# Sparse attention, gate and mixer in one kernel: gate preparation placed inside the mixer of the batch ahead, gate values in tiles of their own, the second batch's convolution mostly on ScalarE and GpSimd

## The chip, the cores and the metric

The kernel runs on one core of a Trainium2 chip. The metric is the time of one execution on the device in microseconds (us); lower is better. PE is TensorE (PEld its weight loads), DVE is VectorE, ACT is ScalarE, POOL is GpSimd and SP is SyncE, whose queue issues the DMAs.

## What is computed

Three stages follow each other. B = 4 batches, H = 8 heads, S = 576 positions, head width 64, model width D = 512. Everything is float32.

```python
# attention: only the 32 largest scores of a row count
scores = 0.125 * q @ k.T                      # [4, 8, 576, 576]
kth    = the 32nd largest of each row
attn   = softmax(where(scores >= kth, scores, -1e9))
x      = attn @ v                             # heads side by side: [4, 576, 512]
# gate: a causal convolution of 5 taps along the positions, per channel
gate   = sigmoid(sum_k conv_w[k] * x[s - 4 + k])
x      = (gate * (x @ w_val)) @ w_out
# mixer
u      = x + (relu(x.T @ w_tok1) @ w_tok2).T
out    = u + relu(u @ w_ch1) @ w_ch2          # inner width 1536
```

## The kernel before

**Attention.** The heads are taken in pairs, 16 in all, four to a batch (`p = 4 b + c`). A pair has five units `u` of 128 rows of each head (the last unit holds 64 rows of both). For a unit, PE computes the scores into PSUM (`scores`, L366, L387, L389), ACT copies them to SBUF (L377, L395), and DVE finds the 32nd largest value of each row: `fold` (L531) halves the row by maxima and minima, `topk` (L544 to L546) takes the best of the halves, and `top32` (L567, L569) runs four rounds of MAX and three of MATCH_REPLACE for each tile. Then ACT forms a large penalty W for scores under the threshold (L469), POOL subtracts it (L471, `E <- S, W`), ACT takes the exponential (L474), PE transposes E (L483), ACT copies the transposes to `pT` (L488), and PE multiplies with v (`pv`, L496 to L501). Two units are held and their products issued in one group; ACT copies the result to `xf[c]` (L504). For the last six pairs the scores are computed early and parked in DRAM through the tiles `pst` (`pre`), which are free again after that.

**Gate preparation.** `prep(b, c)` handles channel block c (128 of the 512 channels) once its pair is done: reciprocal of the row sums (L685 to L696), their spread over the channels by PE (L694, L700, L703) into two of the three PSUM banks `mo`, the multiplication of `xf[c]` by them on DVE (L708, L710), the split of x into a high and a low part (`split`, L586 on ACT, L587 on POOL), and the convolution. For the first batch the convolution is done by PE with diagonal matrices (L723). For the other three it runs in the single PSUM bank Q: for each half of 288 positions ACT writes the first tap (L732), DVE adds four more (L735, each reading and writing Q), and ACT takes the tanh (L737) into the tile `f[c]`.

**Gate and mixer.** All weight products are three passes over high and low parts (`mm3`, L647 to L649). `gate(b)` computes `x @ w_val` (96 passes of 288 columns), DVE combines it with the gate value (L764), the result is split and multiplied by `w_out` (96 more), and ACT writes it to `f[c]` (L770). `mix(b)` transposes `f`, does the two token products, and then G = 3 rounds of four `ch1` blocks with ReLU and four `ch2` blocks, whose sums DVE adds to `f` (L789). So in this kernel the gate values of a batch and the mixer's running result of the batch before stand in the same four tiles `f`. In batches one and two (`b in LO` is false) the low parts of the mixer are formed by ACT and POOL through two tiles `t`, in three and four by DVE.

**Order.** Nothing is issued directly: each step is recorded as an operation with its engine, a cost and the buffers it reads and writes. `Order.issue` then lists all operations by priorities (list scheduling on estimated costs, refined in 8 rounds), to which the table `SHIFT` adds corrections by operation number. Each engine works through its own list strictly in that order. Buffers and PSUM banks are assigned in recording order, so where a step is recorded decides what it has to wait for: in `all`, a batch's four `prep` calls are recorded after its last pair and after the mixer of the batch before, then its `gate`, then its `mix`; attention of the next batch is recorded after that and listed among them by priority. A `check` near the end tests that the shortened selection was valid; a complete version of the program behind a branch is not taken.

## Time and profile before

| what | value |
|---|---|
| time, median of 3 runs | 877.21 us (875.7 to 878.32) |
| profiled execution: time / span | 874.26 us / 872.4 us |
| busy: PE / DVE / ACT / POOL | 820.0 / 743.1 / 602.0 / 386.8 us |
| mean granted TensorE clock | 0.978 of full speed |
| DMA | 139.4 MB, 160 GB/s |
| chain that ended last | PE 62%, DVE 27%, ACT 7% |

The span runs from the first to the last instruction of the profiled execution; the time of that execution also holds what lies around it. Busy time is the union of an engine's instructions. Matmuls overlap in the pipeline and their ends are modelled, so that a stretch in which PE is busy throughout can still hold a few per cent of lost time; what the table of stages shows best is where PE stood still. The granted clock is the share of full speed that TensorE got: 1.0 is 2.4 GHz, and it falls to 1.2 GHz (0.5) for some stretches.

### The profile page before, as it was taken

Reading aid. Unit: us, or ns where it says so; the run is one execution under the profiler, and the core shown is the slowest. Engines: PE = TensorE matmul, PEld = TensorE weight load, DVE = VectorE, ACT = ScalarE, POOL = GpSimd, SP = SyncE. Lnnn points to the kernel's source line nnn. Section 1 sums busy time; section 2 is a strip of 40 time slices with the busy share of each in tenths; the row PEclk is TensorE's granted clock in tenths of the full one; section 3 lists DMA queues with packets and bytes.
Section 4 is the critical chain, followed back from the end, with each engine's and each line's share of the span. In section 5 each row is a group of like instructions: output and inputs, shape, how many; then the busy total and the mean of one; then the engine's idle time right before and its main releaser. Section 6 shows DMA issues by size and latency. Waiting matters only on the chain.

```text
span 872.4 us, 19037 instructions
## 1 busy us (share of the span) xinstructions
PE 820.0 (94%) x6585; PEld 711.0 (81%) x6585; DVE 743.1 (85%) x2786; ACT 602.0 (69%) x1484; POOL 386.8 (44%) x372
## 2 busy tenths in 40 slices
PE   6898897899999999979999999998999999999997
PEld 3564565589789888769798888988899998889997
DVE  7999999999789999999999989999999995623222
ACT  5999999976777759677987778587876655432110
POOL 1344354467676748345784454454354223302000
PEclk8899999999999999979999999999999999999999
DMA  6445445558246764636433336735346645233553
GB/s 236 162 143 178 164 160 187 188 174 302 84 139 220 251 196 155 197 123 186 131 103 90 98 94 198 240 121 172 113 152 206 190 146 151 98 97 96 172 169 107
DMA packets 45835, 139.38 MB, mean 160 GB/s; under 512 B 5216, under 2 KB 5472, under 8 KB 45728
## 3 DMA queue, kind: packets, MB, share of 16 engines
q1 hardware_dynamic: 45728, 138.06, 48.8%
q8 instruction: 54, 0.88, 0.4%
q14 instruction: 53, 0.43, 0.2%
HBM read 100.62 MB, written 37.42 MB: 158 GB/s over the span
## 4 chain that ended last, share of the span: by engine, by line
PE 62%; DVE 27%; ACT 7%; issue 2%; DMA 1%; POOL 1%; SPq 0%; DVEq 0%; ACTq 0%
PE mo L647 14%; PE mo L648 12%; PE mo L649 12%; PE PT L483 5%; DVE top L567 5%; DVE Z L569 5%; PE PT L496 4%; PE Sp L366 4%; DVE Q L735 4%; DVE y L531 3%; DVE X L544 2%; DVE Sp L531 1%; PE mo L366 1%; DVE A L531 1%; ACT E L474 1%
## 5 line engine op out<-in xcount | busy, mean ns | idle before, releaser
L647 PE MATMUL mo<-r,ring 128*128 128x288 f32 x864 | 266.6, 309 | 3.0 <-DVE f L789 1.0
L648 PE MATMUL mo<-r,ring 128*128 128x288 f32 x864 | 255.5, 296 | 0.4 <-POOL r L587 0.2
L649 PE MATMUL mo<-r,ring 128*128 128x288 f32 x864 | 255.3, 296 | 0.0
L471 POOL TENSOR_TENSOR E<-S,W 128x576 f32<-128x576 f32 x144 | 202.8, 1424 | 98.8 <-ACT W L469 63.6
L647 PEld LDWEIGHTS mo<-r,ring 128*128 128x128 f32 x864 | 162.9, 189 | 17.3 <-issue 8.9
L648 PEld LDWEIGHTS mo<-r,ring 128*128 128x128 f32 x864 | 163.1, 189 | 0.9 <-POOL r L587 0.8
L649 PEld LDWEIGHTS mo<-r,ring 128*128 128x128 f32 x864 | 162.9, 189 | 0.0
L567 DVE MAX8 top<-Z 128x8 f32<-128x168 f32 x432 | 127.2, 322 | 0.6
L474 ACT ACTIVATE E<-E,nb 128x576 f32<-128x576 f32 x144 | 112.2, 780 | 14.6 <-POOL E L471 14.2
L483 PE MATMUL PT<-ident,E 128*128 128x128 f32 x656 | 102.8, 286 | 12.9 <-ACT pT L488 5.7
L488 ACT ACTIVATE pT<-PT 128x512 f32<-128x512 f32 (+1 forms) x144 | 94.9, 659 | 28.7 <-PE PT L483 27.7
L469 ACT ACTIVATE W<-S,nb 128x576 f32<-128x576 f32 x144 | 108.2, 776 | 0.3 <-POOL E L471 0.3
L483 PEld LDWEIGHTS PT<-ident,E 128*128 128x128 f32 x656 | 76.9, 145 | 35.9 <-ACT pT L488 12.0
L569 DVE MATCH_REPLACE8 Z<-top,Z 128x168 f32<-128x168 f32 x288 | 89.8, 317 | 0.0
L556 POOL TENSOR_TENSOR bad<-X,top 128x6 f32<-128x6 f32 (+1 forms) x80 | 16.2, 203 | 160.9 <-DVE top L567 142.2
L496 PE MATMUL PT<-pT,v 128*64 128x128 f32 (+1 forms) x640 | 78.9, 266 | 4.1 <-ACT pT L488 3.8
L497 PE MATMUL PT<-pT,v 128*64 128x128 f32 (+1 forms) x640 | 78.9, 266 | 0.0
L496 PEld LDWEIGHTS PT<-pT,v 128*64 128x64 f32 x640 | 64.6, 137 | 15.3 <-ACT pT L488 9.8
L366 PE MATMUL Sp<-qk 64*128 64x288 f32 x320 | 65.4, 481 | 11.5 <-ACT S L377 6.4
L869 ACT ACTIVATE r<-mo 128x288 fp32r<-128x288 f32 x81 | 33.0, 410 | 50.9 <-PE mo L649 50.6
L531 DVE TENSOR_TENSOR y<-S,Sp 128x576 f32<-128x576 f32 (+1 forms) x80 | 54.6, 683 | 14.7 <-PE Sp L366 11.5
L587 POOL TENSOR_TENSOR r<-f,r 128x576 fp32r<-128x576 f32 x32 | 45.4, 1431 | 44.3 <-ACT r L586 44.2
(178 smaller groups left out, 1924.0 us busy)
## 6 DMA issues: line engine op xcount, KB each, us to landing
ring<-ch1d SPq DMA_DIRECT2D x36, 512.0 KB, 3.6
ring<-ch2d SPq DMA_DIRECT2D x36, 512.0 KB, 3.5
sd<-pst SPq DMA_DIRECT2D x54, 288.0 KB, 2.6
S<-sd SPq DMA_DIRECT2D x24, 576.0 KB, 3.9
stage<-in_w_ch_dram SPq DMA_DIRECT2D x24, 512.0 KB, 4.1
ch1d<-ring SPq DMA_DIRECT2D x12, 512.0 KB, 3.9
ch2d<-ring SPq DMA_DIRECT2D x12, 512.0 KB, 2.9
ring<-vald SPq DMA_DIRECT2D x12, 512.0 KB, 4.3
```

The costliest lines, as they stand in the source:

```text
L366: nc.tensor.matmul(bank[t][:, 0:288], q[r, 128 * u:128 * u + 128], k[r, c0:c0 + 288], start=True, stop=True)
L469: self.act(S, lambda W=W, x=x, t=t: nc.scalar.activation(W, x, AF.Relu, bias=nb[:, t, 1:2], scale=-BIG), kx + [(kN, 1)], [kW], True)
L471: self.pool(S, lambda W=W, x=x, E=E: nc.gpsimd.tensor_tensor(E, x, W, op=OP.subtract), kx + [kW], [kE])
L474: self.act(S + 110, lambda E=E, d=d, t=t: nc.scalar.activation(E, E, AF.Exp, bias=nb[:, t, 0:1], scale=0.125, accum_out=d), [kE, (kN, 0)], ...
L483: nc.tensor.transpose(self.PT[:, y * 128:(y + 1) * 128], E2[:, k * 128:(k + 1) * 128], self.ident)
L496: nc.tensor.matmul(o[0:64, 0:n], vt[:, y], a[:, y * 128:y * 128 + n], start=(y == 0), stop=False)
L531: self.dve(w * a.shape[-1], lambda o=o, a=a, b=b, f=f: v.tensor_tensor(o, a, b, op=f), ka, ko)
L567: self.dve(n, lambda src=src, o=o: v.max(o, src), k, [(kM, q)] + [kM] * (q in (0, 3)))
L569: self.repl(n, lambda src=src, o=o: v.match_replace(out=z, in_to_replace=o, in_values=src, imm_value=NEG), k + [(kM, q)], [kz])
L647: nc.tensor.matmul(o, wh, xh, start=(x == 0), stop=False)
L648: nc.tensor.matmul(o, wh, xl, start=False, stop=False)
L649: nc.tensor.matmul(o, wl, xh, start=False, stop=(x == last))
```

## The change

1. `gate values`: for batches two to four `prep` writes the gate value to `pst[c]` (function `gated`) and not to `f[c]`, so it no longer has to wait for the mixer of the batch before.
2. `placement`: `all` records the mixer of batch b - 1 after the attention of batch b, and inside it, through the callback `between`, the preparation of blocks c = 0, 1, 2 of batch b, at three of six points (PLACE: before `ch2` of rounds one, two and three). Block c = 3 comes after the mixer, then `gate(b)`. The splits of x are taken out of `prep` and stand at the head of `gate` for batches two to four (`halves`).
3. `convolution`: for the second batch (b = 1) and c = 0, 1, 2 the taps are five ACT multiplications of 576 columns (scaled copies into `pst[c]` and the two `t` tiles), summed by four POOL additions, with one tanh of 576 columns. Block 3 of that batch and all blocks of the last two batches keep the DVE form.
4. `P V`: the four tiles `pT` become one tile, and the two held units are multiplied by v in one matmul of 256 columns where there were two of 128.
5. `SHIFT` is another table, so positions on all engines move.

```diff
@@ -27,47 +27,27 @@
 WP = ()
 PRE = (3, 0), (3, 1), (3, 2), (3, 3), (2, 0), (2, 1)
 MOFF = (8, 0, -4, 0)
+CADD = 3
+PLACE = 1, 3, 5
 WOFF = 9
-SHIFT = ((6, 1467, "PE", 0.6), (1470, 1475, "PE", -2.9), (1487, 1490, "PE", -13.9), (1494, 1574, "PE", -0.8),
...
+SHIFT = ((1065, 1068, "PE", -2.7), (2359, 2366, "PE", -1.3), (2773, 2777, "PE", -3.7), (3122, 3237, "PE", -24.4),
...
 
 
 class Clock:
@@ -241,7 +221,7 @@
         self.nb = [T(f"nb{i}", [128, 2, 2]) for i in range(3)]
         self.Et = [T(f"E{i}", [128, 2 * S]) for i in range(self.nE)]
         self.Wt = [T(f"W{i}", [128, S]) for i in range(self.nW)]
-        self.pT = [T(f"pT{i}", [128, 640]) for i in range(self.nP)]
+        self.pT = T("pT", [128, 4, 640])
         self.bad = T("bad", [128, NP * 5, 2, 3])
         self.cst, self.flag, self.worst = T("cst", [1, 1]), T("flag", [1, 1], I32), T("worst", [128, 1])
         self.den = [T(f"den{i}", [128, 4, 9]) for i in range(2)]
@@ -475,7 +455,8 @@
                 E, E, AF.Exp, bias=nb[:, t, 0:1], scale=0.125, accum_out=d),
                 [kE, (kN, 0)], [kE, ("den", b % 2, c, 2 * u + t)], True)
 
-            pT, kP = self.pT[j % self.nP], ("pT", j % self.nP)
+            y = 2 * len(self.held) + t if w == 2 else 2
+            pT, kP = self.pT[:, y], ("pT", y)
             z = [0, 1, 2, 3, 4] if w == 1 else [5, 6, 7, 8, 4] if t else [0, 1, 2, 3]
 
             def tr(z=z):
@@ -487,18 +468,21 @@
             self.pe(0.109 * len(z) - 0.081, tr, kE2[0:1] if w == 2 and t == 0 else kE2, kp, 0.1, kind=Order.TURN)
             self.act(n, lambda pT=pT, n=n: nc.scalar.activation(pT[:, 0:n], self.PT[:, 0:n], AF.Copy), kp, [kP])
             pts.append((pT, kP))
-        a, e = pts[0][0], pts[-1][0]
         n = 128 if w == 2 else 64
-        g = 128 - n
-
-        def pv():
+        P = self.pT
+
+        def pv(m):
+            o = self.PT[:, 640:640 + n * m]
+            if w == 2:
+                a, e = (P[:, t:2 * m:2] for t in range(2))
+            else:
+                a = e = P[:, 2:3]
+            g = 128 - n
             for y in range(4):
-                nc.tensor.matmul(o[0:64, 0:n], vt[:, y], a[:, y * 128:y * 128 + n], start=(y == 0), stop=False)
-                nc.tensor.matmul(o[64:128, 0:n], vt[:, 6 + y], e[:, y * 128 + g:y * 128 + 128], start=(y == 0), stop=False)
-
-            x, z = (e, e) if w == 2 else (a, e)
-            nc.tensor.matmul(o[0:64, 0:n], vt[:, 4], x[:, 512:512 + n], start=False, stop=True)
-            nc.tensor.matmul(o[64:128, 0:n], vt[:, 5 if w == 2 else 10], z[:, 512 + g:640], start=False, stop=True)
+                nc.tensor.matmul(o[0:64], vt[:, y], a[:, :, y * 128:y * 128 + n], start=(y == 0), stop=False)
+                nc.tensor.matmul(o[64:128], vt[:, 6 + y], e[:, :, y * 128 + g:y * 128 + 128], start=(y == 0), stop=False)
+            nc.tensor.matmul(o[0:64], vt[:, 4], e[:, :, 512:512 + n], start=False, stop=True)
+            nc.tensor.matmul(o[64:128], vt[:, 5 if w == 2 else 10], e[:, :, 512 + g:640], start=False, stop=True)
 
         def out():
             self.act(n, lambda: nc.scalar.activation(self.xf[c][:, 4 + 128 * u:4 + 128 * u + n], o[:, 0:n], AF.Copy),
@@ -507,7 +491,7 @@
         self.held.append((pv, out, [x[1] for x in pts] + [("v", s)]))
         if u % 2 or u == 4:
             held, self.held = self.held, []
-            self.pe(2.335 if len(held) == 2 else 0.73, lambda: [x[0]() for x in held],
+            self.pe(2.335 if len(held) == 2 else 0.73, lambda: pv(len(held)),
                     [k for x in held for k in x[2]], ["o"], 0.1, 0.88, Order.COLS)
             for x in held:
                 x[1]()
@@ -709,8 +693,9 @@
                  [kX] + kx[0:4], kx[0:4])
         self.dve(64, lambda x=x, Y=Y: nc.vector.tensor_tensor(x[:, 512:576], x[:, 512:576], Y[:, 0:64], op=OP.mult),
                  [kY] + kx[4:], kx[4:])
-        self.split(x, xh[c], xl[c], kx, K("r", c), K("r", c + 4))
-        g, kg = fs[c], K("f", c)
+        if b == 0:
+            self.halves(b, c)
+        g, kg = self.gated(b, c)
         cw = self.cw[:, c * 5:c * 5 + 5]
         if b in CONV:
             mm = [self.bank() for _ in segs]
@@ -726,6 +711,16 @@
             for y, s0, s1 in segs:
                 self.act(288, lambda g=g, m=mm[y][0], s0=s0, s1=s1: nc.scalar.activation(
                     g[:, s0:s1], m[:, 0:288], AF.Tanh, scale=0.5), [mm[y][1]], kg)
+            return
+        if b == 1 and c < CADD:
+            for k in range(5):
+                t, kt = (g, kg) if k == 0 else self.nxt("tf", self.tf)
+                kt = kt if k == 0 else [kt]
+                self.act(S, lambda t=t, k=k: nc.scalar.activation(
+                    t, xf[:, k:k + S], AF.Copy, scale=cw[:, k:k + 1]), kx + ["cw"], kt, True)
+                if k:
+                    self.pool(S, lambda t=t: nc.gpsimd.tensor_tensor(g, g, t, op=OP.add), kg + kt, kg)
+            self.act(S, lambda: nc.scalar.activation(g, g, AF.Tanh, scale=0.5), kg, kg)
             return
         q = self.Q[:, 0:288]
         for y, s0, s1 in segs:
@@ -737,6 +732,14 @@
             self.act(288, lambda g=g, s0=s0, s1=s1: nc.scalar.activation(g[:, s0:s1], q, AF.Tanh, scale=0.5),
                      ["Q"], kg)
 
+    def halves(self, b, c):
+        self.split(self.xf[c][:, 4:], self.rs[c], self.rs[c + 4], [("x", c, t) for t in range(5)], [("r", c)], [("r", c + 4)])
+
+    def gated(self, b, c):
+
+        k = ("pst", c)
+        return (self.pst[c], [k, (k, 0), (k, 1)]) if b else (self.fs[c], [("f", c)])
+
     def gate(self, b, p0):
         nc = self.nc
         fs, rs = self.fs, self.rs
@@ -754,16 +757,19 @@
 
         xh, xl = rs[0:4], rs[4:8]
         gh, gl = rs[8:12], rs[12:16]
+        for c in range(4 if b else 0):
+            self.prio = p0 - 3 + c // 2
+            self.halves(b, c)
         self.prio = p0 - 2
         if b == B - 1:
             self.lend()
         for c in range(4):
             w, kw = self.piece("val", c)
-            g = fs[c]
+            g, kg = self.gated(b, c)
             for m, km, t in [product(n, w, kw, xh, xl, lambda kc: K("r", kc, kc + 4)) for n in range(2)]:
                 self.dve(288, lambda g=g[:, t], m=m: nc.vector.scalar_tensor_tensor(
-                    g, g, 1.0, m, op0=OP.add, op1=OP.mult), [km] + K("f", c), K("f", c))
-            self.split(g, gh[c], gl[c], K("f", c), K("r", c + 8), K("r", c + 12))
+                    g, g, 1.0, m, op0=OP.add, op1=OP.mult), [km] + kg, kg)
+            self.split(g, gh[c], gl[c], kg, K("r", c + 8), K("r", c + 12))
         for c in range(4):
             w, kw = self.piece("out", c)
             for m, km, t in [product(n, w, kw, gh, gl, lambda kc: K("r", kc + 8, kc + 12)) for n in range(2)]:
@@ -788,7 +794,7 @@
 
         self.dve(288, lambda: self.nc.vector.tensor_tensor(u, m, u, op=OP.add), [km] + ku, ku)
 
-    def mix(self, b):
+    def mix(self, b, between):
         nc = self.nc
         p0 = 36 * (b + 1) + OFF
         fs, rs = self.fs, self.rs
@@ -838,6 +844,7 @@
             self.split(x2[c], uh[c], ul[c], K("f", c), K("r", c), K("r", c + 4))
         rh, rl = rs[8:12], rs[12:16]
         for g in range(G):
+            between(2 * g)
             for f in range(4):
                 self.prio = p0 + 14 + 8 * g + f
                 w, kw = self.piece("ch1", g * 4 + f)
@@ -848,6 +855,7 @@
                                             K("r", kc, kc + 4) + kw) for kc in range(4)], km, 288)
                     ms.append((m[:, 0:288], km, s))
                 self.relu(ms, rh[f], rl[f], b in LO, K("r", 8 + f), K("r", 12 + f))
+            between(2 * g + 1)
             for c in range(4):
                 self.prio = p0 + 16 + 8 * g + c
                 w, kw = self.piece("ch2", g * 4 + c)
@@ -922,13 +930,19 @@
                 if b == 0:
                     self.prep(b, p, self.at + OFF)
             self.dp, self.dd, self.da, self.dl = MOFF
+
+            def between(n):
+                if n in PLACE:
+                    c = PLACE.index(n)
+                    self.prep(b, c, 9 * (4 * b + c + 1) + OFF)
+
+            if b:
+                self.mix(b - 1, between)
+                self.prep(b, 3, self.at + OFF)
             if b == B - 1 and fast:
                 self.check()
-            if b:
-                for c in range(4):
-                    self.prep(b, c, self.at + OFF - XOFF[b] * (3 - c))
             self.gate(b, self.at + OFF)
-            self.mix(b)
+        self.mix(B - 1, lambda n: None)
         self.o.issue(SHIFT if fast else ())
 
 
```

By engine, in the program that runs: DVE loses 24 of 96 convolution steps, ACT exchanges 6 first taps and 6 tanh halves for 15 scaled copies and 3 tanh of 576 columns, POOL gains 12 additions of 576 columns, PE has 320 matmuls fewer (those with v of full units, twice as wide), and the DMAs are the same 320.

**DVE, around the last normalisation of the second batch** (`xf_204` before, `xf_201` after; `top`, `X`, `Z`, `y` belong to the selection of the next batch's first units). Before:

```order
L569 MATCH_REPLACE Z_81<-top_84,Z_81 128x168
L735 SCALAR_TENSOR_TENSOR Q<-xf_203,cw,Q 128x288
L708 TENSOR_TENSOR xf_204<-xf_204,mo_214 128x512
L567 MAX top_84<-X_79 128x8
L710 TENSOR_TENSOR xf_204<-xf_204,mo_212 128x64
L569 MATCH_REPLACE Z_81<-top_84,X_79 128x168
```

Now:

```order
L692 TENSOR_TENSOR xf_201<-xf_201,mo_211 128x512
L530 MAX X_80<-y 128x8
L551 MAX top_85<-X_80 128x8 x2
L553 MATCH_REPLACE Z_82<-top_85,X_80 128x168 x2
L694 TENSOR_TENSOR xf_201<-xf_201,mo_209 128x64
L551 MAX top_85<-Z_82 128x8 x2
```

Before, 20 of the batch's 32 convolution steps stand ahead of this normalisation on DVE; now none does, and in their room stands one more unit of the next batch's selection (6 more MAX of `top`, 5 more MATCH_REPLACE, 6 more MAX and 5 more fold steps).

**POOL, in the first mixer's rounds of `ch1`** (`r<-t` are the low parts of the mixer's ReLU, `ring` weights being split, `E` the attention's subtraction, `bad` the check). Before:

```order
L587 TENSOR_TENSOR ring_207<-wa_113,ring_207 128x512
L876 TENSOR_TENSOR r_193<-t_200,r_189 128x576
L876 TENSOR_TENSOR r_194<-t_199,r_190 128x576
L587 TENSOR_TENSOR ring_208<-wa_112,ring_208 128x512
L556 TENSOR_TENSOR bad<-X_80,top_84 128x6
L471 TENSOR_TENSOR E_90<-S_76,W_91 128x576
L471 TENSOR_TENSOR E_90<-S_76,W_92 128x576
```

Now, at the second block's additions:

```order
L884 TENSOR_TENSOR r_191<-t_196,r_187 128x576
L571 TENSOR_TENSOR ring_205<-wa_109,ring_205 128x512
L722 TENSOR_TENSOR pst_70<-pst_70,t_197 128x576
L540 TENSOR_TENSOR bad<-X_80,top_84 128x6
L571 TENSOR_TENSOR ring_202<-wa_110,ring_202 128x512
L451 TENSOR_TENSOR E_90<-S_76,W_91 128x576
L451 TENSOR_TENSOR E_90<-S_76,W_92 128x576
L722 TENSOR_TENSOR pst_70<-pst_70,t_196 128x576
```

One of a block's four additions stands here ahead of a pair of the attention's subtractions, three behind it.

**PE, at the first block's normalisation for the second batch** (`mo<-ident,rhl` transposes the reciprocals). Before, it stands in the last round of the first mixer:

```order
L648 MATMUL mo_213<-r_194,ring_207 128x288
L649 MATMUL mo_213<-r_190,ring_207 128x288
L694 MATMUL mo_212<-ident,rhl 41x128
L496 MATMUL PT<-pT_96,v_66 64x128
L497 MATMUL PT<-pT_93,v_66 64x128
```

Now it stands in a `ch1` product of the first round, and the product with v has 256 columns:

```order
L633 MATMUL mo_209<-r_178,ring_205 128x288
L678 MATMUL mo_211<-ident,rhl 41x128
L631 MATMUL mo_209<-r_179,ring_205 128x288
L632 MATMUL mo_209<-r_183,ring_205 128x288
L633 MATMUL mo_209<-r_179,ring_205 128x288
L482 MATMUL PT<-pT,v_66 64x256
L483 MATMUL PT<-pT,v_66 64x256
```

The preparation moved ahead by most of a mixer, and it takes two of the three `mo` banks out of the products' rotation while DVE reads them.

## Rows read from the trace of the kernel before

**Rows 1.** The page's first part: busy us, share and instructions of each engine.
```profile
PE 820.0 (94%) x6585; PEld 711.0 (81%) x6585; DVE 743.1 (85%) x2786; ACT 602.0 (69%) x1484; POOL 386.8 (44%) x372
```

**Rows 2.** Busy time by stage; the first line names the columns.
```profile
core 0: us, PE busy (x) PEld busy (x) DVE busy (x) ACT busy (x) POOL busy (x), PEclk, DMA share, GB/s
0.00:182.00 182.00, 153.03 (x1113) 99.74 (x1114) 171.94 (x715) 162.89 (x428) 75.47 (x86) 0.93 0.50 173
...
217.00:280.00 63.00, 62.89 (x504) 53.68 (x499) 53.69 (x183) 47.21 (x110) 42.36 (x38) 1.00 0.44 148
280.00:338.00 58.00, 57.60 (x479) 51.81 (x478) 56.86 (x189) 41.04 (x102) 37.68 (x33) 1.00 0.66 221
338.00:402.00 64.00, 57.01 (x482) 49.12 (x482) 63.76 (x239) 49.32 (x118) 32.96 (x32) 0.92 0.48 155
402.00:545.00 143.00, 141.25 (x1215) 125.97 (x1215) 136.01 (x570) 117.88 (x292) 79.97 (x77) 1.00 0.41 124
545.00:615.00 70.00, 66.17 (x577) 62.33 (x575) 69.43 (x263) 50.25 (x124) 32.97 (x31) 0.98 0.57 180
615.00:718.00 103.00, 102.77 (x872) 97.95 (x870) 101.71 (x408) 69.96 (x171) 39.58 (x42) 1.00 0.51 160
718.00:772.00 54.00, 50.82 (x433) 47.71 (x432) 26.92 (x60) 24.93 (x61) 15.72 (x12) 1.00 0.44 132
772.00:873.00 101.00, 93.56 (x674) 90.13 (x672) 28.71 (x63) 16.42 (x36) 5.68 (x4) 0.99 0.40 123
```

**Rows 3.** The chain that ended last, 360 to 400 us: shares, then start, us, piece.
```profile
by line: DVE Q L735 20.6%; PE mo L647 10.5%; PE mo L648 9.2%; PE mo L649 8.9%; DVE Z L569 8.5%; DVE top L567 8.3%; DVE y L531 6.5%; DVE xf L708 6.4%; DVE X L544 4.5%; DVE f L789 4.5%; DVE Sp L531 2.9%; DVE A L531 2.4%; DVE X L531 2.3%; issu
...
359.44 0.66 DVE y L531
...
364.41 0.46 DVE top L567 x2
364.87 0.61 DVE Z L569 x2
...
368.35 0.43 DVE Q L735
```

**Rows 4.** Groups by line on DVE, 338 to 402 us: busy, mean ns, idle before.
```profile
L735 DVE SCALAR_TENSOR_TENSOR Q<-xf,cw,Q 128x288 f32<-128x288 f32 x32 | 16.3, 509 | 0.0
```

**Rows 5.** Timeline of DVE (and one row of POOL) where batches two and four end.
```profile
387.94 0.68 DVE L708 TENSOR_TENSOR xf<-xf,mo 128x512 f32<-128x512 f32 x1
388.78 0.20 DVE L710 TENSOR_TENSOR xf<-xf,mo 128x64 f32<-128x64 f32 x1
389.78 1.44 POOL L587 TENSOR_TENSOR r<-xf,r 128x576 fp32r<-128x576 f32 x1 [4.08 <-ACT r L586]
717.19 0.34 DVE L567 MAX8 top<-Z 128x8 f32<-128x168 f32 x1
748.16 0.21 DVE L710 TENSOR_TENSOR xf<-xf,mo 128x64 f32<-128x64 f32 x1
```

**Rows 6.** Groups by line on POOL, 217 to 402 us.
```profile
L471 POOL TENSOR_TENSOR E<-S,W 128x576 f32<-128x576 f32 x30 | 42.5, 1431 | 8.2 <-ACT W L469 6.2 <-PE PT L483 2.1
```

**Rows 7.** Groups by line on ACT, 217 to 402 us.
```profile
L469 ACT ACTIVATE W<-S,nb 128x576 f32<-128x576 f32 x29 | 21.5, 771 | 0.0
```

**Rows 8.** Timeline of PE: a group of products with v, and what follows it.
```profile
458.58 0.32 PE L496 MATMUL PT<-pT,v 128*64 128x128 f32 x1
...
460.72 0.27 PE L501 MATMUL PT<-pT,v 128*64 128x128 f32 x1
460.92 0.76 PE L366 MATMUL Sp<-qk 64*128 64x288 f32 x4
```

**Rows 9.** Waits of PE over the span: us in total, times, longest.
```profile
PE PT L496 <- ACT pT L488: 3.8, 6, 1.5
...
PE mo L647 <- DVE xf L708: 0.7, 2, 0.5
```

**Rows 10.** Groups by line on DVE over the span: unpacking of a weight block.
```profile
L621 DVE SCALAR_TENSOR_TENSOR Q<-stage,Q 128x512 int32<-128x512 int32 x34 | 23.2, 682 | 0.1
```

39 lines of the change are left out of this document (13 added, 26 removed), and 17 rows, old and new, of the table SHIFT.

## The prediction

> **What bounds the kernel now.** I read the engines' shares first, then the table by stage, then the chain of waits in the stages where PE falls short. PE is busy 94% of the span, DVE 85% [rows 1]; averages over stages with different limits. The table [rows 2] tells them apart. From 0 to 182 us DVE is full (171.9 of 182) and PE is not (153.0): selection of the first four pairs, unpacking of weights. From 217 to 338 and from 402 to 545 PE is full (within 2 us) and DVE has room: 9.3 us idle in 217 to 280, 7.0 in 402 to 545. At the three places where a batch's attention ends and its gate begins it turns round. In 338 to 402 DVE is busy 63.76 of 64 while PE stands still for 7.0 and its granted clock falls to 0.92. In 545 to 615 DVE is busy 69.4 of 70, PE idle 3.8, clock 0.98. In 718 to 772 PE is idle 3.2 with DVE half idle. From 772 on PE alone works.
>
> What holds DVE at those places: in the chain of 360 to 400 us the convolution step L735 is the largest entry, 20.6%, ahead of any matmul line [rows 3], and 32 of them take 16.3 us busy in that stretch [rows 4]. The change takes 24 of these away and spreads most of the other 64 over the mixers before.
>
> So the prize is PE's lost time at the three gates. Its ceiling: 7.0 idle and 0.08 x 64 = 5.1 us of lost clock make 12.1 at the second batch; 3.8 + 0.02 x 70 = 5.2 at the third; 3.2 at the fourth. Together 20.5 us. No more can be had, as PE's work hardly shrinks (below) and the first 182 us have no step of the change that frees DVE.
>
> **Second batch (convolution moved off DVE, preparation early).** A step on the chain takes DVE 0.43 us [rows 3]; 24 make 10.3 us. But its own last normalisation, `xf[3]`, which everything in the gate waits for, does not come 10 us earlier: by the order, 20 of the steps stood ahead of it (20 x 0.43 = 8.6 us), and one more unit of the next batch's selection now does. That unit by the chain's pieces [rows 3]: 6 MAX at 0.23, 5 MATCH_REPLACE at 0.30, a fold of one step of 0.66 and four of about half that, 6 MAX of the halves at 0.2 (an estimate, they are shorter): about 6.2 us. The difference is 2.4 us; with DVE as full as before, the normalisation that ends at 388.98 us [rows 5] would end at 386.6. That is the floor. The ceiling is 12.1. What decides between them is DVE's 9.3 us of idle time in 217 to 280: there PE works off the first mixer while the fifth pair's attention waits for its turn on PE. Now the fifth pair's last product with v stands some 10 us of PE work earlier in PE's list (by the counts of the order and the spacing of the rows), so score buffers come free earlier and DVE starves less. Half of that idle time won makes 4.6 us on top of 2.4. I take **-7**. After the normalisation the path shortens too: gate values of three blocks are ready, so only block 3's eight steps and their two trips through Q remain between.
>
> **Third batch.** DVE keeps all 32 steps, but 24 are recorded in the second mixer, where DVE had the 7.0 us idle. By the order DVE reaches the last normalisation of this batch with 9 steps and one selection unit less behind it: 3.9 + 6.2 = 10 us of DVE work less than before, against a loss of PE of 5.2 us. DVE is then no longer what PE waits for. Ceiling 5.2, floor 0 if the time is lost elsewhere; **-4**.
>
> **Fourth batch.** The last selection ends at 717.5, the last normalisation at 748.4 [rows 5]; in between PE is the one with a backlog. The order now has all of the third mixer ahead of the last product with v, and all of the `w_val` products behind it. Of 32 convolution steps 20 stay behind the last selection (before: 32). Ceiling 3.2, floor 0; **-1.5**.
>
> **What is added.** ACT: 15 scaled copies and 3 tanh of 576 columns at 0.77 us, the row of the same form with a per-partition scalar [rows 7], are 13.9 us, less 6 + 6 halves taken away; ACT is busy 137.6 of 185 us in 217 to 402 [rows 2], so it is covered. Uncovered it would cost at most the difference, about 8 us. POOL: 12 additions of 576 columns; its subtraction of the same shape takes 1.43 [rows 6], so 17.2 us. POOL is busy 113.0 of 185 us in 217 to 402 [rows 2]; with them 130, or 70%. But POOL works strictly in order, and behind an addition that waits for ACT stand the attention's subtractions, then ACT's exponential, PE's transposes. Bounds 0 and 17.2; the order spreads four additions to a block between other work, so I take 0.5.
>
> The products with v: ten pairs of matmuls where there were twenty, each twice as wide. A group takes from 458.58 to 460.92, 2.34 us [rows 8], and the steady spacing of a pair is its columns' time, so nothing is gained by the width. But before, the first unit's half could run while ACT still copied the second's `pT`; now the first matmul waits for both. PE waited for these copies six times, 3.8 us in all [rows 9]; each could grow by half a group, 1.1 us. Bounds -0.3 and +6.4; I take 0.5, since where PE has other things to wait for it costs nothing.
>
> Normalisations inside the mixer hold two of three `mo` banks until DVE has read them. Before, PE lost 0.7 us to such waits [rows 9], with all four in a row; now nine stand alone among products that rotate through the same banks, and DVE's reading can stand behind a selection round (0.46 + 0.61 us, [rows 3]). Bounds 0 and 9 x 1.1 = 9.9; the order leaves 2.0 to 4.7 us of PE work before the first of the two banks is written again, 1.0 of it the spreading matmuls themselves, so I take 0.5.
>
> The head: in the first 182 us DVE unpacks weights a little earlier (8 steps of 0.68, [rows 10], ahead of the first batch's last normalisation, some selection behind it). That batch's gate starts up to 4 us later, and PE has as much more work ahead of it. Counted at 0, bounds -2 and +4.
>
> **The sum.** -7 - 4 - 1.5 + 0.5 + 0.5 + 0.5 = -11. The profiled execution took 874.26 us, so 863.3; the median of the runs is 2.95 above it: 877.21 - 11 = **866 us**.
>
> **A rule against the change.** A subtraction of 576 columns takes POOL 1.43 us [rows 6], while DVE does a tap of 2 x 288 columns in 2 x 0.43 [rows 3]: POOL needs 1.7 times as long. The Trainium skill (GPSIMD Engine Reference, section Engine selection) says to keep elementwise additions with two inputs on VectorE, as GpSimd is about twice as slow; the trace agrees with the ratio, roughly. By that rule the 10.3 us taken from DVE come back as 17.2 us on the way to the second gate and on POOL's queue, and the sum would be that of the first rival below, 881 us.
>
> **Rivals.**
> 1. *Slower: POOL's queue becomes the wait of the first mixer.* Additions wait for ACT's copies through two `t` tiles that the mixer's ReLU uses as well, and the attention's subtractions wait behind them. POOL's idle time before those subtractions was 8.2 us in the stage [rows 6]; once that is used up, each further addition delays a softmax. Price: 17.2 us of additions, less the 8.6 us that DVE no longer spends ahead of the gate, is 8.6 lost; with -4 - 1.5 later and 1 for the other waits, +4: 881. For it: strict order, one pair of tiles. Against: POOL is at 61% there. Chance 0.10.
> 2. *Gain taken back by bank waits.* Nine normalisations cost 9.9 and the products with v another 2 or so, against -12.5: 877, no change. For it: DVE is full, so its reads come late. Against: the 2 to 4.7 us of slack, and 0.7 us of such waits before. Chance 0.08.
> 3. *DVE stays the bound of the second gate.* Only the floor of 2.4 comes there, 4 at the third batch and nothing at the fourth, less 1.5: -5, 872. For it: the selection unit that takes the steps' place. Against: 9.3 us of idle DVE just before. Chance 0.18.
> 4. *All of PE's lost time is recovered.* -20.5: 857. For it: after the second gate PE was full in every stage anyhow, so whatever is won stays won. Against: PE also loses a little at each mixer's start, and orders listed on estimates never fit wholly. Chance 0.14.
>
> **How the numbers follow.** My forecast, a gain of 7 to 15 us, has the other 0.50. A measurement of this kernel tells about 0.3%, 2.6 us, from no change. Faster than that: forecast, rivals 3 and 4, 0.82; within it: rival 2, 0.08; slower: rival 1, 0.10. The range of 8 in 10 runs from 856, half of rival 4, to 877, with all of rival 3 and half of rival 2.
>
> **What would show it.** Right: in the stage at the second gate PE's idle time falls under 3 us and the clock stays near 1.0; the DVE groups there hold 8 convolution steps, and the last normalisation comes 5 to 10 us earlier; the third gate shows PE full; the tail after the last selection is as long as PE's own work. Rival 1 would show as waits of the subtraction E for POOL's additions and DVE idle before its folds; rival 2 as PE waits for `xf` in the mixers; rival 3 as DVE full and the normalisation at 386 or later. The forecast is wrong if the last selection does not end before 715 us.

## The result, and the profile after

The kernel after takes 865.25 us (median of four runs, 863.61 to 868.89), the kernel before 876.99 in the same job: ratio 0.9872, 95% interval 0.9836 to 0.9908. Forecast were 866 us, a gain of 11; measured is 11.7. The total is right. Its distribution over the stages is right only in part.

The profiled execution of the kernel after took 868.89 us (span 867.1), the longest of its four. The page's first part, then the table by stage with the stages of [rows 2]:

```profile
PE 819.0 (94%) x5945; PEld 683.5 (79%) x5945; DVE 731.2 (84%) x2762; ACT 605.1 (70%) x1490; POOL 404.3 (47%) x384
```
```profile
core 0: us, PE busy (x) PEld busy (x) DVE busy (x) ACT busy (x) POOL busy (x), PEclk, DMA share, GB/s
0.00:182.00 182.00, 151.28 (x914) 89.76 (x914) 168.47 (x696) 156.30 (x410) 72.96 (x83) 0.95 0.53 182
...
217.00:280.00 63.00, 63.00 (x462) 52.17 (x461) 51.50 (x175) 49.59 (x115) 45.71 (x40) 1.00 0.46 157
280.00:338.00 58.00, 56.39 (x428) 47.96 (x426) 57.93 (x204) 46.55 (x109) 42.79 (x38) 1.00 0.58 199
338.00:402.00 64.00, 58.27 (x453) 48.66 (x452) 63.86 (x248) 53.99 (x131) 44.68 (x42) 1.00 0.58 189
402.00:545.00 143.00, 141.24 (x1068) 119.71 (x1067) 133.63 (x545) 111.72 (x278) 76.47 (x73) 1.00 0.38 117
545.00:615.00 70.00, 69.72 (x567) 65.20 (x566) 69.51 (x268) 55.06 (x139) 39.64 (x37) 1.00 0.66 211
615.00:718.00 103.00, 102.53 (x789) 93.14 (x789) 101.95 (x409) 70.43 (x175) 38.10 (x40) 1.00 0.49 155
718.00:772.00 54.00, 53.52 (x415) 50.42 (x412) 27.32 (x69) 24.75 (x58) 16.01 (x13) 1.00 0.50 149
```

Against [rows 2], PE is now full where the third and the fourth batch change from attention to gate: 69.72 of 70 (66.17 before) and 53.52 of 54 (50.82). At the second gate, 338 to 402, the clock is 1.00 where it was 0.92, but PE still stands 5.7 us (7.0 before) and DVE is as full as it was. From 217 to 280 DVE idles 11.5 us; before it was 9.3.

DVE's timeline at the milestones of [rows 5]: the last normalisation of batches one, two and four, and the last selection.

```profile
190.92 0.22 DVE L694 TENSOR_TENSOR xf<-xf,mo 128x64 f32<-128x64 f32 x1
394.73 0.21 DVE L694 TENSOR_TENSOR xf<-xf,mo 128x64 f32<-128x64 f32 x1
724.02 0.33 DVE L551 MAX8 top<-Z 128x8 f32<-128x168 f32 x1
741.64 0.20 DVE L694 TENSOR_TENSOR xf<-xf,mo 128x64 f32<-128x64 f32 x1
```

The second gate's normalisation ends at 394.9, later than the 389.0 before, and the last selection at 724.3, later than 717.5. Both are later because the head of this execution, up to the first `w_out` product, was 7.9 us longer (table below); counted from that product, the last selection ends 1.1 us earlier. From the last selection to the end of the span after takes 142.8 us where it was 154.8: PE has 8.8 us less busy time left there (136.1 against 144.9) and stands 3.3 us less.

To compare executions, the span is cut at PE's first product with `w_out` of each batch, read from PE's timeline (before 200.8, 400.9, 593.1, 758.6; after 208.7, 410.0, 590.3, 753.7). All profiled runs of this study, in us between cuts:

| kernel | head | to 2nd gate | to 3rd | to 4th | rest | median (ratio to before, 95%) |
|---|---|---|---|---|---|---|
| before | 200.8 | 200.1 | 192.2 | 165.5 | 113.8 | 876.99 |
| after | 208.7 | 201.3 | 180.3 | 163.4 | 113.4 | 865.25 (0.9836 to 0.9908) |
| e1 after, P V apart | 206.6 | 201.3 | 180.4 | 163.4 | 113.4 | 866.71 (0.9858 to 0.9904) |
| e2 before, P V merged | 204.8 | 200.0 | 194.6 | 165.4 | 113.9 | 875.81 (0.9972 to 1.0003) |
| e3 after, head of before | 205.7 | 203.7 | 180.3 | 163.7 | 114.0 | 869.28 (0.9894 to 0.9939) |
| e4 before, head of after | 211.9 | 199.2 | 196.9 | 165.5 | 113.6 | 888.41 (1.0108 to 1.0171) |
| e5 one unit's scores early | 207.7 | 201.7 | 180.6 | 163.3 | 113.3 | 867.18 (0.9872 to 0.9914) |
| e6 convolution on DVE | 207.4 | 212.9 | 180.3 | 163.3 | 113.6 | 879.47 (1.0008 to 1.0044) |
| e7 additions twice | 206.1 | 218.4 | 180.4 | 163.4 | 113.4 | 883.8 (1.0053 to 1.0101) |
| e8 batches 3, 4 late | 207.7 | 201.8 | 198.4 | 171.3 | 116.6 | 894.36 (1.0167 to 1.0216) |
| e9 before, offload alone | 203.4 | 211.2 | 189.5 | 165.5 | 114.1 | 885.94 (1.0064 to 1.0139) |
| e10 batch 3 offloaded too | 203.2 | 201.2 | 180.5 | 162.6 | 113.7 | 865.69 (0.9841 to 0.9917) |
| e11 sixth pair early | 206.1 | 200.7 | 180.3 | 163.3 | 113.7 | 863.94 (0.9822 to 0.9877) |
| e12 relisted | 208.0 | 198.4 | 183.9 | 157.2 | 114.4 | 864.12 (0.9824 to 0.987) |

The head varies between executions of one order: 200.8 to 204.8 in before, e2 and e9, which share it; 203.2 to 208.7 in after, e1, e5 to e8, e10 and e11, which share the other. The later columns vary less (163.3 to 163.4 in six of these eight up to the fourth gate), although the third stage of before and e2 is 192.2 and 194.6. So they, not the spans of two single executions, show where time went: with the means of the heads (203.0 and 206.7) and of before and e2 (193.4) in the third, the change costs 3.7 in the head and 1.2 up to the second gate, and gains 13.1 up to the third, 2.1 up to the fourth and 0.4 after. The sum is a gain of 10.7.

The cuts do not part equal work, however. How much attention PE does in a stage can be told from the transposes of E (L483 before, L464 after). The rows are for before and then for after, up to the second, third and fourth gate. A row gives the stage, its length, PE's busy time with these transposes and in brackets their number (one that straddles a cut is counted on both sides), then clock, DMA share and GB/s:

```profile
200.82:400.94 200.12, 23.91 (x155) 0.97 0.55 184
400.94:593.10 192.16, 29.45 (x194) 0.99 0.45 138
593.10:758.60 165.50, 19.50 (x133) 1.00 0.49 153
```
```profile
208.74:409.97 201.23, 25.78 (x173) 1.00 0.56 187
409.97:590.31 180.34, 24.68 (x168) 1.00 0.46 142
590.31:753.68 163.37, 20.92 (x142) 1.00 0.50 155
```

After does 18 more of them up to the second gate, 23 fewer up to the third (three of before's 194 began ahead of the cut) and 9 more up to the fourth. The products with v moved in the same way: e1, which computes them in the form of before, has one group of two units more in the second stage, two fewer in the third and one more in the fourth. With 0.11 us for a further transpose in a row (five take 0.71 us, four 0.60) and 2.34 us for a group [rows 8] this makes, as an estimate, 4.3 us more of PE's work, 7.2 less and 3.3 more. For equal work the change then gains about 3 us up to the second gate, 6 up to the third and 5 up to the fourth. By this estimate over half of what the table shows in the third stage is attention that was done ahead of the second gate or put off behind the third.

### The profile page after: what moved, and what is told of

It is laid out like the page before. It is cut to its first block, busy times and chain, and to the rows that moved or that the text cites. A ratio compares the mean times of both kernels' runs of the same rounds, so it can differ in the third digit from the quotient of the medians.

```text
span 867.1 us, 17746 instructions
## 1 busy us (share of the span) xinstructions
PE 819.0 (94%) x5945; PEld 683.5 (79%) x5945; DVE 731.2 (84%) x2762; ACT 605.1 (70%) x1490; POOL 404.3 (47%) x384
## 4 chain that ended last, share of the span: by engine, by line
PE 60%; DVE 30%; ACT 6%; issue 2%; POOL 1%; DMA 1%; SPq 0%; DVEq 0%; ACTq 0%
PE mo L631 12%; PE mo L633 11%; PE mo L632 11%; DVE top L551 6%; DVE Z L553 6%; PE PT L464 5%; DVE y L515 4%; PE PT L482 4%; PE Sp L346 4%; DVE X L528 3%; DVE Sp L515 2%; DVE A L515 2%; DVE X L515 1%; PE mo L346 1%; ACT E L454 1%
## 5 line engine op out<-in xcount | busy, mean ns | idle before, releaser
L632 PE MATMUL mo<-r,ring 128*128 128x288 f32 x864 | 254.8, 295 | 0.5 <-POOL r L571 0.5
L631 PEld LDWEIGHTS mo<-r,ring 128*128 128x128 f32 x864 | 162.3, 188 | 18.4 <-issue 10.4
L632 PEld LDWEIGHTS mo<-r,ring 128*128 128x128 f32 x864 | 162.5, 188 | 0.9 <-POOL r L571 0.7
L464 PE MATMUL PT<-ident,E 128*128 128x128 f32 x656 | 101.4, 283 | 9.6 <-ACT pT L469 4.3
L464 PEld LDWEIGHTS PT<-ident,E 128*128 128x128 f32 x656 | 76.5, 143 | 31.2 <-ACT pT L469 12.3
L346 PE MATMUL Sp<-qk 64*128 64x288 f32 x320 | 66.2, 488 | 15.5 <-ACT S L357 9.1
L482 PE MATMUL PT<-pT,v 128*64 128x256 f32 (+1 forms) x384 | 74.3, 337 | 4.1 <-ACT pT L469 3.6
L483 PE MATMUL PT<-pT,v 128*64 128x256 f32 (+1 forms) x384 | 74.3, 337 | 0.0
L482 PEld LDWEIGHTS PT<-pT,v 128*64 128x64 f32 x384 | 41.7, 138 | 30.2 <-ACT pT L469 9.1
L528 DVE MAX8 X<-y 128x8 f32<-128x288 f32 x144 | 65.0, 452 | 0.0
```

Of the source, the lines that this page charges most:

```text
L346: nc.tensor.matmul(bank[t][:, 0:288], q[r, 128 * u:128 * u + 128], k[r, c0:c0 + 288], start=True, stop=True)
L464: nc.tensor.transpose(self.PT[:, y * 128:(y + 1) * 128], E2[:, k * 128:(k + 1) * 128], self.ident)
L482: nc.tensor.matmul(o[0:64], vt[:, y], a[:, :, y * 128:y * 128 + n], start=(y == 0), stop=False)
L631: nc.tensor.matmul(o, wh, xh, start=(x == 0), stop=False)
L632: nc.tensor.matmul(o, wh, xl, start=False, stop=False)
```

## The experiments

**Products with v (e1, e2).** The width of the products undone in after, and put alone into before:

```diff
-        def pv(m):
-            o = self.PT[:, 640:640 + n * m]
+        def pv(i):
+            o = self.PT[:, 640 + n * i:640 + n * i + n]
...
-            self.pe(2.335 if len(held) == 2 else 0.73, lambda: pv(len(held)),
+            self.pe(2.335 if len(held) == 2 else 0.73, lambda: [pv(i) for i in range(len(held))],
```

> The kernel after, with each unit's product with v by itself again (matmuls of 128 columns instead of 256); order list and correction table unchanged. Theory (products with v are worth about nothing): 865 +- 2.5 us, ratio to after between 0.997 and 1.003. Rival (the wider matmuls saved several us of PE time; the group of them was busy 78.9 us before and 74.3 after): 869 to 871. Rival (waiting for both copies costs, up to the 6.4 us of the upper bound): 859 to 863.

> The kernel before, with the products with v of a pair of units merged to 256 columns, nothing else. Theory (worth about nothing): 877 +- 2.5 us. Rival (several us of PE time saved): 872 to 874. Rival (waiting for both copies costs): 879 to 883.

Both came out as the theory has it: each interval covers its base kernel's ratio. The stages agree to 0.1 us (e1, after the head). The merging is worth nothing that can be measured.

**The head (e3, e4).** The order of the first 1450 operations, up to the end of the first gate, exchanged between the kernels:

```diff
+            prio[0:len(HEAD)] = HEAD
             start, end = self.list_schedule(succ, np, prio, True)
```

> The kernel after, where the 1450 operations up to the end of the first gate, which are the same in both kernels, are given the order that they have in the kernel before; all later operations keep theirs. In the profiled pair the kernel after had lost 8.7 us more of PE's time by the first gate (58.3 against 49.6 us), which is above the +4 that the prediction set as the bound of the head. Theory A (the order of the head costs this): 857 to 861 us, with the first batch's last normalisation at 183 instead of 191 us. Theory B (the head differs from execution to execution, since DMA arrival decides it, or the lead is lost again at the second gate where DVE is full): 863 to 868 us.

> The kernel before, with the order that the kernel after has in the 1450 operations up to the end of the first gate. Theory A (that order costs 4 to 8 us): 881 to 885 us. Theory B (it makes no difference to the end): 875 to 879 us.

Neither run bears out a theory: e3 is slower than both of its theories allow, e4 slower than its theory A. In before, after's head costs 11.5 us (8.9 in the head against the mean, 3.5 up to the third gate). In after, before's head gains nothing: its head column is 1.0 shorter than the mean (the first batch's last normalisation ends at 186.9, not at 183), the next 2.4 longer. A head's order is good only together with what follows it. What in e4 makes it so dear was not traced.

**DVE's idle time at the first mixer (e5, e11).** The longest wait of DVE in after, from its timeline (in brackets: idle time before, and what ended it), and PE's timeline there:

```profile
233.51 0.34 DVE L551 MAX8 top<-Z 128x8 f32<-128x168 f32 x1
239.42 0.76 DVE L515 TENSOR_TENSOR y<-S,Sp 128x576 f32<-128x576 f32 x1 [5.57 <-ACT pT L469]
```
```profile
228.73 0.48 PE L631 MATMUL mo<-r,wtok 128*128 128x512 f32 x1
...
235.95 0.39 PE L632 MATMUL mo<-r,wtok 64*128 64x512 f32 x1
235.96 0.51 PE L346 MATMUL Sp<-qk 64*128 64x288 f32 x1
```

The bracket names an ACT copy of another tile, but the fold reads scores: their product L346 stands behind 7.2 us of token products, and PE finished its second half at 239.30. e5 lists this one unit's scores six product groups earlier; e11 lists the whole attention of the sixth pair 10 us earlier.

```diff
+MORE = ((1664, 1667, "PE", -5.4), (1665, 1666, "ACT", -6.0))
...
-        self.o.issue(SHIFT if fast else ())
+        self.o.issue(SHIFT + MORE if fast else ())
```

> The kernel after, with one unit's score products (the ones that DVE waits 5.6 us for at 234 to 239 us) put ahead of the last six products of the token mixer in PE's list, and their copy out of PSUM on ScalarE earlier to match. Theory A (DVE bounds the second gate: from 240 to 402 us it is never idle, so its idle time before that is what sets the gate): the second batch's last normalisation comes 3.5 to 5.5 us earlier than 394.9 - that is at 389.4 to 391.4 when the head is the same - and, as PE is full in most of what follows, the end 3 to 5 us earlier: 860 to 862. Theory B (PE's own backlog bounds the second gate, DVE's wait is only a symptom): normalisation and end unchanged, 864 to 867.

> The kernel after with the whole attention of the sixth pair (scores, selection, softmax, products with v, on four engines) listed 10 us earlier against the first mixer's work. Moving one unit's scores only moved DVE's wait on to the next unit (idle by 260 us: 14.7 us after 217 instead of 11.3 - 11.6 in all by 280 in both). Theory A (it is PE's order in 217 to 260 that starves DVE, and PE has 7.3 us idle in 280 to 402 to take up what is put off): DVE's idle time from 217 to 280 falls from 11.7 to under 6 us, the last normalisation of batch two comes 2.5 to 6 us earlier, 859 to 863. Theory B (both engines' work is needed at that gate, and what PE puts off comes back as a wait): 865 to 870.

From 217 to 280, e5 and then e11:

```profile
217.00:280.00 63.00, 63.00 (x458) 51.56 (x457) 52.61 (x178) 48.63 (x113) 45.19 (x39) 1.00 0.45 151
```
```profile
217.00:280.00 63.00, 62.14 (x454) 50.30 (x452) 55.69 (x196) 52.28 (x125) 44.26 (x40) 1.00 0.43 143
```

In e5 DVE idles 10.4 us, nearly as long as in after: the wait went to the next unit. In e11 it idles 7.3, 4.2 less, but the second gate comes only 0.6 us sooner. From the first batch's last normalisation to the second's it is 204.3 us in e5 and 203.2 in e11, 203.8 in after. By the stages theory B holds in both, although e5's time lies 0.2 us above its range and e11's between the ranges of A and B: in this stretch PE is full or nearly so, and what it does for DVE earlier it does for the mixer later. Nor does all of DVE's idle time there hang on PE: 4.1 us of it in after, 3.1 in before, are waits for weights from DRAM (`stage`). The interval of e11 overlaps that of after.

**Who computes the convolution, and when (e6, e9).** e6 is after with the three blocks on DVE, in place in `pst`; e9 is before with the three blocks on ACT and POOL, late, as its preparation was. e6 and e8 to e12 give the scheduler a whole list of places (`PRIO`) instead of the `SHIFT` table.

```diff
-                if k:
-                    self.pool(S, lambda t=t: nc.gpsimd.tensor_tensor(g, g, t, op=OP.add), kg + kt, kg)
...
+            for k in range(1, 5):
+                self.dvep(S, lambda k=k: nc.vector.scalar_tensor_tensor(
+                    g, xf[:, k:k + S], cw[:, k:k + 1], g, op0=OP.mult, op1=OP.add), kx + kg, kg)
```

> The kernel after with blocks 0 to 2 of batch two's convolution on DVE again, still inside the first mixer: 12 steps of 576 columns take the place of 12 ScalarE copies and 12 GpSimd additions; all other operations keep their places. By the step of 512 columns (0.69 us) a step of 576 is about 0.77 us, so DVE gets 9.2 us. Theory A (DVE bounds the second gate): the end comes 7 to 9 us later, 872 to 874, nearly all of the change's gain. Theory B (the gain comes from where the preparation stands, not from who computes it): 865 to 868.

> The kernel before with blocks 0 to 2 of batch two's convolution computed as the change computes them (ScalarE copies, GpSimd additions, whole blocks of 576), but where the preparation stood before: behind the first mixer, all four blocks close to the gate; all other operations keep their places. Theory A (the offload pays only because the blocks come early: doubling GpSimd's part cost the kernel after 17.5 us, so there is no room left on that queue, and here its 17 us would fall into the last 35 us before the gate): 880 to 886, slower than before. Theory B (24 steps of 0.43 us less on DVE, which bounds that gate, pay by themselves): 867 to 871.

e6, groups on DVE from 217 to 410:

```profile
L698 DVE SCALAR_TENSOR_TENSOR pst<-xf,cw,pst 128x576 f32<-128x576 f32 x12 | 12.2, 1020 | 0.0
```

A step of 576 columns takes 1.02 us, not the 0.77 estimated, so DVE got 12.2 us; the second gate came 11.6 later (212.9 against 201.3) and no later stage changed. The order list and the work in each stage are those of after, so like is compared with like. Theory A, though the time lies above its range: DVE bounds that gate, and its work counts nearly in full. e9, the stage at the second gate, POOL's group from 360 to 415, and waits of PE from 338 to 415:

```profile
338.00:402.00 64.00, 50.89 (x412) 42.06 (x411) 60.47 (x251) 55.57 (x129) 46.53 (x45) 0.85 0.40 131
```
```profile
L695 POOL TENSOR_TENSOR f<-f,t 128x576 f32<-128x576 f32 x12 | 16.8, 1406 | 0.1
```
```profile
PE PT L440 <- ACT E L431: 5.5, 3, 2.7
PE mo L657 <- ACT rT L653: 3.7, 1, 3.7
```

Here DVE has 3.5 us to spare, and PE waits for ACT: the slower time that e9's theory A expected. The early place without the offload is 2.7 us slower than before (e6; 0.7 to 3.9 by its interval), the offload without the early place 8 slower (e9), both together 11.7 faster. Each half keeps the order list of the program that it was cut from; neither was listed anew, so an ill-fitting order can be part of what each loses.

**POOL's queue (e7).** Each addition followed by one more of its shape:

```diff
+                        nc.gpsimd.tensor_tensor(g, g, t, op=OP.add)
+                        nc.gpsimd.tensor_tensor(t, g, t, op=OP.subtract)
...
```

> The kernel after with each of the 12 additions on GpSimd followed by a second operation of the same shape on the same tiles (a subtraction whose result nothing reads): GpSimd gets 17 us more in 235 to 365 us, at the places where the change put its work. Theory A (GpSimd's queue has room; the prediction's 0.5 us): 865 to 867. Rival (the attention's subtractions wait behind the additions, and the softmax, ScalarE and the scores' buffers behind them): 869 to 882.

The stages of e7, and the longest waits of DVE (338 to 402) and of ACT (280 to 402):

```profile
280.00:338.00 58.00, 49.57 (x352) 41.30 (x351) 51.82 (x181) 40.30 (x95) 46.51 (x40) 0.93 0.50 171
338.00:402.00 64.00, 54.63 (x385) 44.53 (x386) 55.13 (x211) 48.51 (x116) 47.24 (x42) 0.95 0.50 169
```
```profile
DVE y L515 <- ACT S L375: 4.3, 1, 4.3
DVE A L515 <- ACT S L375: 3.3, 1, 3.3
```
```profile
ACT pst L726 <- POOL t L724: 8.7, 3, 3.5
ACT E L454 <- POOL E L451: 8.4, 12, 1.9
```

17 us more on POOL cost 17.1 us at the second gate, though POOL is busy at most 80% there. ACT waits for POOL at the tanh and at the exponential, its copies of scores stand behind, and DVE, which is busy 63.86 of 64 us there in after, waits for those. In after ACT never waits for POOL at that tanh, and at the exponential for 4.5 us from 217 to 402, 4.6 in before. So the change's own additions are hidden, but in these places they use the cover up. e7 does not part the queue from the tiles: the second operation also holds its tile `t` and the block's tanh longer, and ACT's copies wait 2.9 us for a `t`.

**Where the preparation of batches three and four stands (e8, e10).** e8 records it behind the mixer again; e10 leaves it early and takes batch three's blocks 0 to 2 off DVE too (`b in (1, 2)`).

```diff
-                if n in PLACE:
+                if n in PLACE and b < 2:
...
-                self.prep(b, 3, self.at + OFF)
+                for c in range(3 if b < 2 else 0, 4):
+                    self.prep(b, c, self.at + OFF)
```

> The kernel after with the preparation of batches three and four behind the mixer again, at about the distances that they had in the kernel before; batch two as in the change. Theory A (the early preparation is what fills PE at the third and fourth gates): the end comes 5.5 to 10 us later, 871 to 875, PE idle again at both gates. Theory B (the third and fourth gates gain only because the order was listed anew): 864 to 868.

> The kernel after with blocks 0 to 2 of batch three's convolution on ScalarE and GpSimd as well; all other operations keep their places. DVE has 24 steps of 0.43 us less (10.3 us), GpSimd 17 us more, in the stretch from 470 to 555 us. Theory A (at the third gate PE is full - 69.7 of 70 us - and DVE's time there is worth nothing any more; DVE is idle 9.4 us in 402 to 545 anyway): 863.5 to 867. Theory B (DVE, full from 545 to 718, still bounds the last selections): 857 to 862. Rival C (GpSimd's queue costs as much as in the run with the additions doubled): 875 to 883.

e8, third and fourth gate:

```profile
545.00:615.00 70.00, 64.00 (x467) 55.79 (x466) 67.45 (x252) 48.02 (x122) 34.13 (x32) 0.90 0.54 166
718.00:772.00 54.00, 51.00 (x378) 46.51 (x376) 27.34 (x71) 22.00 (x53) 12.84 (x12) 0.94 0.40 116
```

PE stands and the clock falls at both, as theory A says (the fourth window ends ahead of e8's own fourth cut at 779.2; from cut to cut PE stands 10.6 us at a clock of 0.97), but the price is 29 us, not 5.5 to 10: 18.1 up to the third gate, 7.9 up to the fourth, 3.2 after. Against before's own order the same stages are 5.0 (198.4 to 193.4), 5.8 and 2.8 longer, 13.6 in all; this much at least is an order that fits the late place badly. That leaves the gain of the three stages itself, 15.6, for the early place together with its order, and no run parts these two. In e10, 10.3 us less on DVE change nothing up to the third gate and 0.8 up to the fourth: its theory A. DVE no longer bounds there. Nor do the 17.1 us of additions that POOL gets there cost anything.

**The best version (e12).** The two small candidates together, and the order list fitted further by single moves on the scheduler's estimates:

```diff
-        if b == 1 and c < CADD:
+        if b in (1, 2) and c < CADD:
...
-        self.o.issue(SHIFT if fast else ())
+        self.o.issue(PRIO if fast else ())
```

> The kernel after with batch three's blocks 0 to 2 on ScalarE and GpSimd too, the sixth pair's attention earlier, and the places of single stretches of operations in the order list then moved by small steps, kept where the kernel's own list scheduler, from its estimates of durations, ended no later (its own end 9 us earlier than for the kernel after). No operation differs from those of the run with batch three's convolution moved. Theory A (what is left at the gates and in the head is a matter of the order, and the estimates are good enough to find it; they foresaw the sign of the runs before): 856 to 861. Theory B (the two lone changes were worth 0.6 us each by their stages, so the second gate is held by DVE's and PE's work together, and an order fitted to estimates does not carry over to the chip): 863 to 868.

Nine estimated us gave 864.12: theory B. The second and fourth stages are 2.9 and 6.2 shorter than in after, the third 3.6 longer; again work moved (182 transposes of E in the third, 128 in the fourth), and PE is never idle between the second and the fourth cut. e11 and e12 beat before clearly (ratios 0.9849 and 0.9847), but after by no more than the intervals allow.

## Why the prediction was right, point by point

- **Second batch, -7: too much; DVE's part of it came out as in rival 3.** The last normalisations of batches one and two lie 203.8 us apart, 206.1 before: 2.3 us won, the floor of 2.4. The step that failed is "Half of that idle time won makes 4.6 us on top". DVE's idle time between the two went from 11.6 up to 15.3 us, and its work down by 6.0:

```profile
182.89:388.98 206.09, 198.53 (x1612) 173.95 (x1613) 194.49 (x670) 150.08 (x358) 127.78 (x114) 0.98 0.57 190
```
```profile
191.14:394.94 203.80, 196.46 (x1464) 166.58 (x1465) 188.48 (x673) 161.51 (x377) 148.67 (x130) 1.00 0.54 181
```

  The path behind the normalisation, expected to shorten, is longer: 15.0 us to the first `w_out` product where it was 12.0. PE does not stand there in either kernel:

```profile
388.98:400.94 11.96, 11.96 (x91) 11.73 (x90) 11.96 (x38) 7.61 (x18) 7.64 (x7) 1.00 0.55 165
```
```profile
394.94:409.97 15.03, 15.03 (x118) 13.85 (x118) 15.03 (x60) 9.97 (x24) 8.79 (x8) 1.00 0.57 169
```

  The difference is attention of the next batch: 14 transposes of E and a group of products with v, against 4 transposes. That is why the table shows a loss of 1.2 where, for equal work, about 3 us are won. What e5 and e11 add: where PE is full, a DVE wait is not worth its length, even when it is removed. The clock did return to 1.00 and eight convolution steps remain on DVE there, as foreseen, but PE's idle time stayed at 5.7, not under 3. The steps taken from DVE are nonetheless worth 11.6 us (e6), more than the 10.3 that the prediction counted from the chain.

```profile
L730 DVE SCALAR_TENSOR_TENSOR Q<-xf,cw,Q 128x288 f32<-128x288 f32 x8 | 4.1, 512 | 0.0
```

- **Third batch, -4: right in mechanism, and for equal work a little small.** Measured are 11.9 us in the profiled pair and 13.1 with e2, about 7 of which are attention done elsewhere; the rest, 5 to 6, is at or just over the ceiling of 5.2. In the window of that ceiling, 545 to 615, PE's idle time fell from 3.8 to 0.3 us and the clock rose from 0.98 to 1.00, as foreseen. By milestones, 5.3 us lie from the second batch's last normalisation to the third's (187.0 to 181.6), 3.4 from there to `w_out` (17.1 to 13.7), and 3.1 are those just ahead. The second passes of the weight products (L648 before, L632 after) in 560 to 600 show that a PE counted as busy can be busy with other things than the gate:

```profile
560.00:600.00 40.00, 12.17 (x40) 0.96 0.55 180
```
```profile
560.00:600.00 40.00, 24.15 (x82) 1.00 0.66 209
```

  The gate's and mixer's products run twice as densely: 82 second passes where there were 40. Of the 40 us PE stood 3.8 before and none after; the rest it spent before on attention (45 transposes of E, 27 after) and on the spreading of row sums (four blocks, one after). The 10 us of DVE work less that the step started from measured 7.5:

```profile
388.98:575.96 186.98, 183.96 (x1558) 166.68 (x1557) 179.49 (x725) 146.59 (x361) 103.80 (x97) 0.99 0.46 140
```
```profile
394.94:576.58 181.64, 179.88 (x1377) 156.67 (x1377) 172.03 (x692) 141.88 (x354) 100.94 (x94) 1.00 0.44 136
```

- **Fourth batch, -1.5:** 2.1 by the table, about 5 for equal work, more than the ceiling of 3.2; PE's idle time from cut to cut fell from 5.1 to 0.8 us. The marker "before 715 us" for the last selection failed (724.3): it assumed that what is won shows as an earlier end of selection, but that end moves with the head (1.1 us earlier when counted from the first cut), and what is won is that PE has less work left then.
- **POOL's additions, +0.5:** right, with 17.3 us of additions as estimated (17.2), but the cover was thinner than "70% busy" suggested: e7 shows the next 17 us in the same places at full price, with the waits that rival 1 named. POOL's groups from 217 to 402:

```profile
L451 POOL TENSOR_TENSOR E<-S,W 128x576 f32<-128x576 f32 x34 | 48.1, 1427 | 9.8 <-ACT W L449 9.8
...
L722 POOL TENSOR_TENSOR pst<-pst,t 128x576 f32<-128x576 f32 x12 | 17.3, 1439 | 0.3
```

- **The rule against the change** (the Trainium skill, GPSIMD Engine Reference, section Engine selection: additions with two inputs belong on VectorE). Like against like the trace agrees with the page's "about two": two inputs of 576 columns took 0.74 us on DVE before (`fold`, L531) and 1.42 on POOL, a ratio of 1.9. But a tap is one multiply-add on DVE, 1.02 us (e6), and 1.44 on POOL for its addition alone, a ratio of 1.4; the prediction's 1.7 took 0.43 us for a half step, the piece on the chain, where the busy time is 0.51 [rows 4]. Which engine bounds the stage decides: the rule's choice, e6, reaches the second gate 11.6 us later than after; in e9, where POOL's additions stand late, close to the gate, the time is 8 us longer than before, as the rule would have it.
- **P V, +0.5, and bank waits, +0.5:** nothing speaks against them. (Six waits of 1.1 are a bound of 6.6, not 6.4; nothing hangs on it.) Waits of PE in after, to be held against [rows 9]:

```profile
PE PT L482 <- ACT pT L469: 3.6, 5, 1.1
...
PE mo L708 <- DVE xf L692: 0.4, 1, 0.4
```

- **The head, 0:** +3.7 by the means, near its upper bound of +4. The order of the head alone does not give it back (e3).
- **The sum.** By the cuts -7 became +1.2, 0 became +3.7, -4 became -13.1 and -1.5 became -2.1; for equal work, by the estimate above, the three gates gave about -3, -6 and -5. The errors cancel either way, so that the total came within 1 us is luck. The range held because it was bounded by PE's lost time as a whole, while the terms were tied to the gate at which the cause lies instead of the stage in which PE gets the time back. Left open is how much of the gain is the new order list by itself: no run lists before anew.

## What to carry to other kernels

Work taken from an engine that is full and work put early paid only together here, in the order lists that were run: each half alone lost. Part of the gain shows one stage later, because attention moved across the cuts; count the work between two marks before you compare the time between them. An engine's busy share says little on what it can still take: with two scratch tiles and strict queues, POOL at 133.2 of 185 us (217 to 402) had nothing left for another 17 in the same places, while in the next stage, where it is busy 87.7 of 143 us with them (402 to 545), 17 us more were free (e10). Compare stages between fixed marks over several executions, since a single pair of spans would have shown half of this gain.

## What the runs showed that was not expected

The first 200 us of the same order vary by up to 5.5 us between executions (203.2 to 208.7), while each later stage of after's order repeats within 0.5 us where the steps are the same; the third stage of before's order does not (192.2 and 194.6). The cause was not looked for. A DVE step of 288 columns that reads and writes PSUM takes 0.51 us, one of 576 columns in SBUF 1.02: the time per column was the same in both.
